# A fused attention and SoLU layer on one core: w_in's load moved ahead of chunk 1, late stores split over two queues, a new hand-off order

## Chip, core and metric

The kernel runs on one core of a Trainium2 chip. The metric is the time of one execution on the device in microseconds (us). Engines are named as in the profile: PE (TensorE, matmuls; PEld is its weight load), DVE (VectorE), ACT (ScalarE), POOL (GpSimd) and SP (SyncE, which here only issues DMAs). POOL and ACT issue DMAs as well.

## What is computed

```python
# q, k, v: (8, 8, 576, 64); w_in: (512, 1024); w_out: (1024, 512), all float32
kv = einsum('bhsd,bhse->bhde', k, v)
out = einsum('bhsd,bhde->bhse', q, kv)
x = out / sqrt(mean(out * out, -1) + 1e-6) * g_norm      # -> (4608, 512), heads side by side
h = x @ w_in
sm = softmax(h)                                          # with + 1e-9 in the denominator
solu = h * sm
ln = (solu - mean(solu)) / sqrt(var(solu) + 1e-6) * g_ln
y = ln @ w_out                                           # (4608, 512)
```

## The kernel before

The 4608 tokens are worked in nine chunks of 512. Chunks 0 to 7 take eight of every nine rows of one batch each (a partition holds nine rows in succession); chunk 8 (`LAST`) collects every ninth row of all batches, out of `q_last`. The kernel is a set of named steps, made by `add(name, engines, function, needs, uses)`. The string `ORDER` lists every step once, written out; `Plan.emit` walks it and issues each step on its engine, so every engine works through its own steps in exactly that order and never passes a step that waits. `word:act` in ORDER chooses ACT where a step may run on two engines. `HOME` gives each PSUM tile one of eight banks; two tiles of one bank follow each other, the second waits for the last reader of the first. `kept` gives the number of SBUF buffers by kind, and a load into a buffer waits for its last reader.

The steps of a chunk c, with the line of the profile that carries them:

- Loads `q.c`, `k.c`, `v.c` by POOL's DMA queue, which casts float32 to bf16 (L318). Chunks 0 and 1 come in halves of four heads (`HALVES`: `k.0.1` is the second half of chunk 0's k). The first halves of chunk 0 are loaded as float32 by SP (`ld.v`, `ld.k`, `ld.q`, L328) and cast by an engine (`v.0.0` and so on, L232). `w_in.0`, `w_in.1` are the halves of w_in (rows 0 to 255 and 256 to 511, L342), `w_out.0`, `w_out.1` those of w_out (L347). `gs` and `g_all` are small loads of the gains.
- `kv_mm` (L378) forms k-transposed times v; the `kv` steps copy it to bf16 (L232). `qT_mm` and `qT` transpose q by PE and copy it out (L416, L232); for chunks 5 to 8 (`XBAR`) one DMA transpose does it (`qT.5`, L425). `o_mm` (L444) multiplies the two.
- `sq` squares o (ACT, L236), `s_mm` (L508) takes the mean over each head, `ex` is the reciprocal root (ACT; chunk 0 in one step, L522, the others as Ln and Exp, `ln` L512 and `ex` L516), `x` multiplies it in (DVE, L528). For chunks 6 to 8 (`TOKA`) the same is done token by token: `o_mm` L458, `sq`, `ssum` (POOL), `sred` (DVE), `rh` (ACT), `rg` (POOL), `xt` (DVE), and a DMA transpose `x.c` (L500).
- `h.c.f` is x times w_in. In chunks 0 to 2 (`SPLIT`) `h.c.f.0` uses the first two of four blocks of the contraction (x's first half of heads, w_in.0) and `h.c.f.1` the last two (L583). `exp` (ACT, L590), `u` = h times exp (DVE, L594), `usq` (POOL or ACT) and `es` (POOL, L607) follow, then `sums` (PE, L694), `turn` and `stats` (DVE) and `rstd` (ACT). Chunks 4 to 8 (`TOKS`) keep tokens on the partitions: `h.c.m.g` (L612), `expt` (ACT, L620), `ut` (DVE, L626), `bn` (DVE, L632), `stats`, `rstd`, and a DMA transpose `turnu.c.half` (SP, L648) that gives the stationary operand of the last product.
- `w_mean` (PE, L741) and `w_center` (DVE, L746) fold g_ln and the mean into w_out, once.
- `out.c.m.part` is the product with w_out (L760), `ob` scales it by rstd (DVE L244 or ACT L242), `store` writes it out (L785, L788 and L783), all of them on SP but some of chunk 8. In chunks 6 and 7 one `store` issues two DMAs of 64 rows.

`warm.n` are filler matmuls on zeros (L824); `FILL` gives for each the bank that it writes, how many matmuls, and their columns.

## Time and profile before

| what | before |
|---|---|
| median of 3 runs | 183.58 us (183.0 to 183.73) |
| the profiled execution: its time | 184.51 us |
| its span, from the first to the last instruction | 182.4 us |
| busy: PE, DVE, ACT, POOL | 171.9, 133.5, 135.6, 98.0 us |
| first matmul of chunk 0's h | 20.80 us |
| end of the last matmul | 177.40 us |
| matmuls of `warm`: number, busy | 49, 14.80 us |
| HBM read, written | 32.54 MB, 9.44 MB |

Times inside the trace count from the first instruction of the span. The DMA share of a stretch can pass 1, since it sums the packets' own times. A row of the timeline gives the start, the duration, the engine and line, the operation with out<-in and shapes, how many are merged, and in brackets the idle time of that engine before it with what ended it.

### The profile page before, as it was taken

The page shows a single profiled execution, that of the slowest core. Times are in us where ns is not written, and L with a number is a line of the kernel's source. Part 1 is how long each engine was busy: PE and PEld are TensorE (multiplying, and loading weights), DVE is VectorE, ACT ScalarE, POOL GpSimd, SP SyncE. Part 2 cuts the span into 40 slices and gives each one's busy share as a digit, 9 for nine tenths or more (in the row PEclk, how much of TensorE's full clock was granted, in tenths as well). Part 3 has the DMA queues.
Part 4 walks back from the last instruction along what each step waited for, and adds up shares of the span by engine and source line. Part 5 has one row for each costly group of instructions (what it writes and reads, how often), then busy time and mean ns, then how long its engine had stood idle before and what let it go on. Part 6 is the DMA issues. An engine that isn't in the chain of part 4 may idle for free.

```text
span 182.4 us, 5075 instructions
## 1 busy us (share of the span) xinstructions
PE 171.9 (94%) x2057; PEld 83.7 (46%) x2074; DVE 133.5 (73%) x277; ACT 135.6 (74%) x279; POOL 98.0 (54%) x112
## 2 busy tenths in 40 slices
...
GB/s 188 291 213 211 207 313 324 205 210 207 209 207 269 244 207 209 207 193 149 254 131 91 167 127 156 114 205 202 218 167 163 252 262 185 208 140 216 207 239 170
DMA packets 56139, 37.10 MB, mean 203 GB/s; under 512 B 37548, under 2 KB 49332, under 8 KB 56116
## 3 DMA queue, kind: packets, MB, share of 16 engines
...
HBM read 32.54 MB, written 9.44 MB: 230 GB/s over the span
## 4 chain that ended last, share of the span: by engine, by line
PE 56%; DVE 12%; DMA 3%; ACT 1%; issue 1%
PE out_ps L760 22%; PE h_ps L612 17%; PE h_ps L583 8%; DVE bn_sb L632 4%; DVE u_sb L626 4%; DMA w_sb<-u_sb 3%; PE misc_ps L378 2%; PE misc_ps L694 2%; PE s_ps L508 2%; PE o_ps L444 1%; PE misc_ps L416 1%; DVE x_sb L528 1%; PE o_ps L458 1%; DVE w_out_sb L746 1%; DVE usq_sb L496 1%
## 5 line engine op out<-in xcount | busy, mean ns | idle before, releaser
L612 PE MATMUL h_ps<-w_in_sb,x_sb 128*128 128x512 bf16 x153 | 37.0, 379 | 0.8 <-DVE usq_sb L496 0.4
L760 PE MATMUL out_ps<-w_out_sb,w_sb 128*128 128x512 bf16 (+1 forms) x166 | 36.8, 369 | 0.6 <-DMA w_sb<-u_sb 0.3
L238 POOL TENSOR_TENSOR usq_sb<-u_sb 128x512 bf16<-128x512 bf16 x29 | 29.8, 1042 | 9.9 <-PE s_ps L508 6.4
L620 ACT ACTIVATE e_sb<-h_ps,zero_t 128x512 f32<-128x512 f32 x40 | 27.2, 687 | 8.5 <-PE h_ps L612 7.7
L583 PE MATMUL h_ps<-x_sb,w_in_sb 128*128 128x512 bf16 x128 | 30.4, 379 | 1.4 <-DVE x_sb L528 1.4
L760 PE MATMUL out_ps<-w_out_sb,u_sb 128*128 128x512 bf16 x120 | 30.4, 379 | 0.5
L594 DVE TENSOR_TENSOR u_sb<-h_ps,e_sb 128x512 bf16<-128x512 f32 x32 | 20.9, 685 | 8.8 <-ACT e_sb L590 8.7
L626 DVE TENSOR_TENSOR u_sb<-h_ps,e_sb 128x512 bf16<-128x512 f32 x40 | 26.0, 680 | 1.6 <-ACT e_sb L620 1.5
L632 DVE BATCH_NORM_STATS2 bn_sb<-u_sb 128x6 f32<-128x512 bf16 x40 | 25.8, 681 | 0.2
L760 PEld LDWEIGHTS <-w_sb 128*128 128x128 bf16 x168 | 16.3, 98 | 18.7 <-DMA w_sb<-u_sb 0.8
L612 PEld LDWEIGHTS <-x_sb 128*128 128x128 bf16 x160 | 15.4, 98 | 19.0 <-issue 1.2
L528 DVE SCALAR_TENSOR_TENSOR x_sb<-o_ps,g_cols,rst_sb 128x512 bf16<-128x512 f32 x24 | 18.8, 794 | 7.0 <-ACT rst_sb L516 3.8
L590 ACT ACTIVATE e_sb<-h_ps,zero_t 128x512 f32<-128x512 f32 x32 | 20.6, 691 | 4.2 <-PE h_ps L583 4.0
L607 POOL TENSOR_TENSOR es_sb<-e_sb 128x512 bf16<-128x512 f32 x16 | 20.2, 1274 | 2.2 <-ACT e_sb L590 2.2
L583 PEld LDWEIGHTS <-w_in_sb 128*128 128x128 bf16 x128 | 11.9, 98 | 15.8 <-issue 3.2
L760 PEld LDWEIGHTS <-u_sb 128*128 128x128 bf16 x128 | 11.9, 98 | 14.0 <-issue 0.8
L236 ACT ACTIVATE osq_sb<-o_ps,zero_t 128x512 bf16<-128x512 f32 x24 | 15.5, 682 | 3.4 <-PE o_ps L444 3.4
L489 POOL TENSOR_TENSOR lss_sb<-rh_sb,g_all 128x512 f32<-128x512 f32 x12 | 12.3, 1043 | 7.9 <-ACT rh_sb L485 7.9
L473 POOL TENSOR_TENSOR es_sb<-rst_sb 128x512 f32<-128x512 bf16 x6 | 6.9, 1157 | 15.3 <-ACT rst_sb L236 8.9
L512 ACT ACTIVATE lss_sb<-s_ps,eps_t 128x512 f32<-128x512 f32 x20 | 13.6, 685 | 1.7 <-PE s_ps L508 1.6
L516 ACT ACTIVATE rst_sb<-lss_sb,zero_t 128x512 f32<-128x512 f32 x20 | 14.5, 723 | 0.4
L232 DVE CAST kvd<-misc_ps 64x128 bf16<-64x128 f32 (+1 forms) x23 | 6.4, 288 | 9.1 <-PE misc_ps L378 7.7
...
## 6 DMA issues: line engine op xcount, KB each, us to landing
q_sb<-in_q_dram POOLq DMA_DIRECT2D x6, 576.0 KB, 18.1
k_sb<-in_k_dram POOLq DMA_DIRECT2D x6, 576.0 KB, 18.1
...
```

Of the source, the lines that this page charges most:

```text
L236: nc.scalar.activation(out=dst, in_=src, func=AF.Square, bias=zero_t[:, :])
L238: on[engine].tensor_tensor(out=dst, in0=src, in1=src, op=MUL)
L528: nc.vector.scalar_tensor_tensor(out=t[:, z, 2 * hf:2 * hf + 2].rearrange("p a (vt w) -> p w (a vt)", w=2), in0=T["o", c, hf, z].rearrange ...
L583: nc.tensor.matmul(bank(("h", c, f), [128, 512])[:, :], w_in_sb[:, dt, f * 128:(f + 1) * 128], T["x", c][:, :, dt, :], start=(dt == 0), st ...
L590: nc.scalar.activation(out=t[:, f % 2, :], in_=T["h", c, f][:, :], func=AF.Exp, bias=zero_t[:, :])
L594: nc.vector.tensor_tensor(out=t[:, f, :], in0=T["h", c, f][:, :], in1=T["e", c, f // 2][:, f % 2, :], op=MUL)
L607: on[engine].tensor_tensor(out=t[:, n, :], in0=e[:, 0, :], in1=e[:, 1, :], op=ADD)
L612: nc.tensor.matmul(bank(("h", c, m, g), [128, 512])[:, :], x[:, NP * (m ^ 2 * odd(c, dt)) + dt, :] if c in TOKA else x[:, m // 2 ^ odd(c, ...
L620: nc.scalar.activation(out=t[:, g, :], in_=T["h", c, m, g][:, :], func=AF.Exp, bias=zero_t[:, :], accum_out=se[:, m, g:g + 1])
L626: nc.vector.tensor_tensor(out=t[:, m, g * 512:(g + 1) * 512], in0=T["h", c, m, g][:, :], in1=T["e", c, m][:, g, :], op=MUL)
L632: nc.vector.bn_stats(out=t[:, m, g, :], in_=T["u", c][:, m, g * 512:(g + 1) * 512])
L760: nc.tensor.matmul(bank(key, [128, d_model])[:, cols], T["w", c][:, m, f, :] if c in TOKS else T["u", c][:, f, m * 128:(m + 1) * 128], w_o ...
```

## The change

In ORDER, SP loads `ld.v`, `ld.q`, `ld.k` one behind the other and then the small gains; POOL makes `ident` first, then loads `k.0.1`, `v.0.1`, `q.0.1`, then both halves of w_in, and only then chunk 1 and w_out; chunk 3's q comes ahead of chunk 2's. Chunk 0's first half of heads is worked first, then its second half. ACT casts v and q of that half, DVE casts k. The stores of chunks 6 and 7 become two steps each, `store.c.m.0` (64 rows) on SP and `store.c.m.1` on ACT (`store_part`), and stores of chunks 4 and 5 may go by ACT as well: ACT issues 17 stores instead of 3. The order of all other steps, the PSUM banks (`HOME`, all lines replaced) and the fillers (`FILL`, 44 matmuls instead of 49, 19 instead of 27 ahead of the first transposes) are new. The suffix "!" that FILL's words may have is not used in this FILL.

```diff
@@ -18,101 +18,102 @@
 ORDER = """
-warm.6 warm.3 ld.v q.0.1 ld.k k.0.1 v.0.1 ident warm.2 v.1.0 warm.0 q.1.0 qT_mm.0.1 v.0.0 k.0.0:act kv_mm.0.0 kv.0.0.0
-kv.0.0.1:act warm.1 k.1.0 qT.0.1:act gs w_in.0 w_in.1 k.1.1 ld.q q.0.0 qT_mm.0.0 warm.4 q.1.1 qT.0.0 kv_mm.0.1 turn_g
-o_mm.0.0 q_last.0:act sq.0.0.1 kv.0.1.1 kv.0.1.0 warm.7 s_mm.0.0.1 sq.0.0.0 ex.0.0.1 o_mm.0.1 sq.0.1.1 sq.0.1.0 g_ln
-s_mm.0.0.0 x.0.0.1 v.1.1 ex.0.0.0 warm.8 s_mm.0.1.1 ex.0.1.1 x.0.0.0 x.0.1.1 w_out.0 warm.12 s_mm.0.1.0 qT_mm.1.0
-qT.1.0 w_out.1 q.2.0 k.2.0 ex.0.1.0 x.0.1.0 v.2.0 kv_mm.1.0 kv.1.0.1:act kv.1.0.0:act warm.9 h.0.7.0 table h.0.1.0
-warm.5 h.0.4.0 o_mm.1.0 sq.1.0.0 sq.1.0.1 k.3.0 h.0.5.0 g_mean h.0.6.0 h.0.4.1 exp.0.4 u.0.4 usq.0.4 h.0.1.1 exp.0.1
-h.0.6.1 u.0.1 usq.0.1 h.0.5.1 exp.0.5 es.0.2 u.0.5 usq.0.5 exp.0.6 u.0.6 h.0.0.0 h.0.0.1 exp.0.0 u.0.0 q.3.0 usq.0.0
-s_mm.1.0.1 ln.1.0.1 ex.1.0.1 qT_mm.1.1 qT.1.1 usq.0.6 x.1.0.1 h.0.2.0 h.0.2.1 exp.0.2 u.0.2 s_mm.1.0.0 ln.1.0.0
...
-bn.8.2.0 turnu.8.0 out.7.0.0 out.7.0.1 ob.6.1:act out.7.2.0 store.6.1 bn.8.1.1 out.7.2.1 stats.7 rstd.7 out.7.3.0
-out.7.3.1 bn.8.0.1 ob.7.1 bn.8.1.0 ob.7.2:act store.7.2 out.8.2.0 out.8.2.1 out.8.1.0 out.8.1.1 out.8.0.0 out.8.0.1
-out.8.3.0 bn.8.0.0 bn.8.2.1 ob.7.3:act store.7.1 ob.7.0:act stats.8 rstd.8 ob.8.2:act ob.8.1:act store.7.3
-store.8.1:act ob.8.0:act store.8.0:act store.7.0 store.8.2 ob.8.3.0:act store.8.3.0 out.8.3.1 ob.8.3.1:act
-store.8.3.1:act
+ld.v ld.q ident k.0.1 ld.k k.0.0 v.0.1 gs v.0.0:act warm.0 q.0.0:act q.0.1 qT_mm.0.0 kv_mm.0.0 kv.0.0.1:act
+kv.0.0.0:act qT.0.0 warm.1 warm.2 o_mm.0.0 g_all w_in.0 w_in.1 v.1.0 sq.0.0.0 q.1.0 k.1.0 v.1.1 q.1.1 k.1.1 turn_g
+g_ln g_mean sq.0.0.1 kv_mm.0.1 s_mm.0.0.0 warm.3 s_mm.0.0.1 w_out.0 ex.0.0.1 kv.0.1.0 kv.0.1.1:act ex.0.0.0 qT_mm.0.1
+qT.0.1 warm.4 warm.5 o_mm.0.1 sq.0.1.0 warm.6 warm.7 s_mm.0.1.0 w_out.1 x.0.0.1 sq.0.1.1 x.0.0.0 h.0.7.0 h.0.3.0
+h.0.4.0 q.3.0 q.2.0 q_last.0:act ex.0.1.0 x.0.1.0 s_mm.0.1.1 ex.0.1.1 x.0.1.1 table h.0.6.0 h.0.1.0 h.0.0.0 h.0.2.0
+h.0.2.1 exp.0.2 h.0.3.1 exp.0.3 es.0.1 u.0.3 usq.0.3 h.0.4.1 exp.0.4 u.0.4 k.2.0 u.0.2 h.0.7.1 exp.0.7 u.0.7 v.2.0
+h.0.6.1 exp.0.6 u.0.6 usq.0.6 es.0.3 usq.0.4 h.0.1.1 exp.0.1 u.0.1 q_last.1 usq.0.1 qT_mm.1.0 qT.1.0:act usq.0.7
+h.0.5.0 h.0.5.1 exp.0.5 es.0.2 h.0.0.1 v.3.0 kv_mm.1.0 kv.1.0.1:act exp.0.0 es.0.0 kv.1.0.0 warm.8 warm.9 o_mm.1.0
+sq.1.0.1 warm.10 warm.11 s_mm.1.0.1 u.0.0 usq.0.0 u.0.5 usq.0.5 qT_mm.1.1 qT.1.1 sq.1.0.0 s_mm.1.0.0 ln.1.0.0
+kv_mm.1.1 kv.1.1.0 kv.1.1.1 warm.12 warm.13 o_mm.1.1 ln.1.0.1 ex.1.0.1 x.1.0.1 ex.1.0.0 x.1.0.0 k.3.0 k.5.0 v.5.0
+w_mean.0 sq.1.1.1 warm.14 s_mm.1.1.1 h.1.0.0 sq.1.1.0 ln.1.1.1 s_mm.1.1.0 ln.1.1.0 h.1.5.0 h.1.3.0 ex.1.1.0 x.1.1.0
+h.1.2.0 ex.1.1.1 x.1.1.1 w_mean.1 w_center.0 w_center.1 w_center.2 w_center.3 usq.0.2:act h.1.6.0 w_center.5 h.1.4.0
+h.1.4.1 h.1.6.1 exp.1.6 u.1.6 h.1.3.1 exp.1.3 exp.1.4 u.1.3 h.1.2.1 exp.1.2 u.1.4 h.1.0.1 exp.1.0 u.1.0 q.4.0 h.1.5.1
+usq.1.3 exp.1.5 u.1.5 u.1.2 usq.1.6 usq.1.2 sums.0 turn.0 w_center.4 qT_mm.3.0 qT.3.0:act usq.1.4:act es.1.2 out.0.0.0
+out.0.0.1 usq.1.5:act h.1.7.0 h.1.7.1 exp.1.7 es.1.3 u.1.7 stats.0 h.1.1.0 h.1.1.1 exp.1.1 u.1.1 es.1.0 out.0.3.0
+out.0.3.1 usq.1.1 es.1.1 qT_mm.2.0 qT.2.0:act k.4.0 qT_mm.3.1 usq.1.0 qT.3.1 out.0.3.2 kv_mm.2.0 kv.2.1.1:act
+kv.2.1.0:act kv.2.0.2 kv.2.0.1:act kv.2.0.0:act kv.2.1.2 rstd.0 qT_mm.2.1 qT.2.1 w_center.6 out.0.1.0 v.4.0 out.0.1.1
+out.0.0.2 w_center.7 o_mm.2.0 sq.2.0.1 o_mm.2.1 out.0.1.2 out.0.1.3 ob.0.1 out.0.3.3 ob.0.3 sq.2.0.0 usq.1.7
+s_mm.2.0.0 k.7.0 sq.2.1.0 ln.2.0.0 ex.2.0.0 out.0.0.3 ob.0.0 sq.2.1.1 s_mm.2.0.1 ln.2.0.1 ex.2.0.1 warm.15 kv_mm.3.0
+kv.3.1.2 kv.3.1.1 kv.3.1.0 kv.3.0.1:act out.0.2.0 v.7.0 out.0.2.1 out.0.2.2 x.2.0.0 v.6.0 kv.3.0.0 s_mm.2.1.0 ln.2.1.0
...
+ut.7.3.0 out.6.1.0 expt.7.0.0 ob.5.3:act out.6.1.1 bn.6.2.0 stats.6 ut.7.1.1 ut.7.0.0 x.8 h.8.2.1 bn.7.3.0 out.5.2.1
+turnu.7.0 bn.7.1.0 rstd.6 ob.6.2:act ob.6.1:act bn.7.2.1 expt.8.2.1 h.8.2.0 store.6.1.1 ut.8.2.1 out.6.0.0 out.6.0.1
+ut.7.2.0 h.8.3.1 h.8.1.0 expt.8.2.0 ut.8.2.0 expt.8.3.1 h.8.1.1 store.6.1.0 h.8.3.0 store.5.3:act bn.7.2.0 expt.8.1.1
+bn.8.2.0 bn.7.1.1 store.6.2.1 expt.8.3.0 store.2.3 h.8.0.1 expt.8.0.1 bn.7.3.1 store.6.2.0 ut.8.3.1 ut.8.3.0
+ob.5.2:act turnu.7.1 store.5.2 h.8.0.0 bn.8.3.1 ob.6.0:act ut.8.0.1 expt.8.0.0 bn.7.0.0 stats.7 out.6.3.0 ut.8.0.0
+out.6.3.1 ob.6.3:act turnu.8.1 expt.8.1.0 bn.8.2.1 ut.8.1.0 store.2.0 out.7.0.0 rstd.7 ut.8.1.1 bn.8.0.1 store.6.0.0
+turnu.8.0 out.7.1.0 out.7.1.1 bn.8.0.0 out.7.0.1 ob.7.0:act store.7.0.1 out.7.2.0 out.7.2.1 store.6.3.1 out.7.3.0
+out.7.3.1 ob.7.1 bn.8.1.0 store.7.1.1 store.6.0.1 store.7.0.0 store.7.1.0 out.8.2.0 out.8.2.1 ob.7.2 store.7.2.1
+out.8.1.0 out.8.1.1 ob.7.3:act store.7.3.0 out.8.0.0 bn.8.1.1 store.7.3.1 store.6.3.0 out.8.0.1 bn.8.3.0 stats.8
+rstd.8 ob.8.1 out.8.3.0 ob.8.2:act store.8.2:act store.8.1:act ob.8.0:act store.8.0:act store.7.2.0 out.8.3.1
+ob.8.3.1:act ob.8.3.0 store.8.3.1:act store.8.3.0
 """
...
 HOME = """
...
 """
...
-FILL = {0: ("s.warm", 19, 512), 1: ("misc.qT.0.0", 5, 512), 2: ("o.0.0.1", 5, 512), 3: ("o.0.1.1", 2, 512), 4: ("s.0.1.1", 1, 512), 5: ("h.0.4", 1, 512), 6: ("h.0.6", 1, 512), 7: ("s.0.0.1", 4, 512), 8: ("s.0.1.1", 2, 512), 9: ("h.0.7", 4, 512), 10: ("s.1.1.1", 1, 512), 11: ("h.1.1", 3, 512), 12: ("s.0.1.0", 1, 512)}
+FILL = {0: ("s.warm", 19, 512), 1: ("o.0.0.0", 2, 512), 2: ("o.0.0.1", 1, 512), 3: ("s.0.0.1", 1, 512), 4: ("o.0.1.0", 3, 512), 5: ("o.0.1.1", 1, 512), 6: ("s.0.1.0", 3, 512), 7: ("h.0.7", 1, 512), 8: ("o.1.0.0", 2, 512), 9: ("o.1.0.1", 1, 512), 10: ("s.1.0.1", 3, 512), 11: ("misc.qT.1.1", 1, 512), 12: ("o.1.1.0", 3, 512), 13: ("o.1.1.1", 1, 512), 14: ("s.1.1.1", 1, 512), 15: ("misc.kv.3.0.0", 1, 512)}
@@ -771,6 +772,10 @@
         t = kept_tile(ob_key(c, m), [128, d_model], FP32)
         times(engine, t[:, cols], T[key][:, cols], T["rstd", c][:, m:m + 1])
 
+    def store_part(engine, c, m, x):
+        rows = out[c * S:c * S + S, :].rearrange("(p j) d -> p j d", j=9)
+        on[engine].dma_start(rows[:, 4 * (m % 2) + m // 2 + 2 * x, :], T[ob_key(c, m)][64 * x:64 * x + 64, :])
+
     def store(engine, c, m, cols):
         t = T[ob_key(c, m)]
         first = 4 * (m % 2) + m // 2
@@ -781,11 +786,8 @@
                 on[engine].dma_start(last, t[:, cols])
             else:
                 on[engine].dma_start(out.rearrange("(r j) d -> j r d", j=9)[8, 128 * m:128 * m + 128, cols], t[:, cols])
-        elif c not in TOKA:
+        else:
             on[engine].dma_start(rows[:, first:first + 3:2, :], t[:, :])
-        else:
-            for x in range(2):
-                on[engine].dma_start(rows[:, first + 2 * x, :], t[64 * x:64 * x + 64, :])
 
     all_cols = slice(0, d_model)
     for c in range(NC):
@@ -808,7 +810,11 @@
                     [("w_center", f) for f in fs] + ([("turnu", c, m // 2)] if c in TOKS else [("u", c, f) for f in fs])
                     + ([("out", c, m, part - 1)] if part else []), [("w" if c in TOKS else "u", c), key])
             add(("ob", c, m), "dve|act", lambda e, key=key: scale(e, key, all_cols), [("out", c, m, n_parts - 1), ("rstd", c)], [key, ob_key(c, m), ("rstd", c)])
-            add(("store", c, m), "sp|act" if c == LAST else "sp", lambda e, c=c, m=m: store(e, c, m, all_cols), [("ob", c, m)], [ob_key(c, m)])
+            if c in TOKA and c < B:
+                for x in range(2):
+                    add(("store", c, m, x), ("sp", "act")[x], lambda _, a=(c, m, x): store_part(("sp", "act")[a[2]], *a), [("ob", c, m)], [ob_key(c, m)])
+                continue
+            add(("store", c, m), "sp|act" if c >= 4 else "sp", lambda e, c=c, m=m: store(e, c, m, all_cols), [("ob", c, m)], [ob_key(c, m)])
 
     def warm(key, n, cols):
         kind = key[1] if key[0] == "misc" else key[0]
@@ -827,10 +833,11 @@
 
     by_word = {plan.word(key): key for key in plan.users}
     for n, (word, count, cols) in FILL.items():
-        key = by_word.get(word, ("s", "warm"))
-        if key in plan.users:
-            plan.pieces[plan.users[key][0]][2].append(("warm", n))
-        add(("warm", n), "pe", lambda _, a=(key, count, cols): warm(*a), [], [key])
+        key, over = by_word.get(word.rstrip("!"), ("s", "warm")), word.endswith("!")
+        users = list(plan.users.get(key, []))
+        if users and not over:
+            plan.pieces[users[0]][2].append(("warm", n))
+        add(("warm", n), "pe", lambda _, a=(key, count, cols): warm(*a), users if over else [], [key])
 
     plan.settle(HOME)
     plan.emit(ORDER)
```

## The prediction

> **What bounds the kernel now.** I read first the head of the page and the busy time by stretches of the span (columns: length, then busy time of PE, its weight loads, DVE, ACT and POOL, granted clock, DMA share, GB/s), then the same view for the filler matmuls of L824 alone, then the timeline of the first 30 us.

> ```profile
> span 182.4 us, 5075 instructions
> 9.69:22.75 13.06, 12.06 (x293) 6.42 (x294) 6.51 (x12) 8.03 (x14) 4.66 (x7) 1.00 1.18 209
> 22.75:60.00 37.25, 35.51 (x487) 18.31 (x487) 27.35 (x50) 31.92 (x56) 35.40 (x38) 1.00 1.22 244
> 60.00:120.00 60.00, 59.47 (x935) 29.70 (x941) 48.65 (x95) 55.03 (x114) 38.67 (x40) 1.00 0.94 173
> 120.00:170.00 50.00, 49.25 (x283) 22.40 (x288) 48.33 (x102) 33.38 (x86) 11.76 (x12) 1.00 0.96 201
> 177.40:182.40 5.00, 0.00 (x0) 0.00 (x0) 0.00 (x0) 0.47 (x1) 0.00 (x0) 0.79 0.52 177
> 9.69:22.75 13.06, 5.05 (x18) 1.51 (x18) 1.00 1.18 209
> 20.80 1.02 PE L583 MATMUL h_ps<-x_sb,w_in_sb 128*128 128x512 bf16 x4 [0.46 <-DVE x_sb L528]
> 22.75 3.63 PE L583 MATMUL h_ps<-x_sb,w_in_sb 128*128 128x512 bf16 x16
> ```

> From 22.75 us on PE is busy for 35.51 of 37.25, 59.47 of 60 and 49.25 of 50 us: it is the bound, and no order of the same matmuls can take much out of that part. DVE (48.33 of 50 from 120 to 170 us) stands right beside it. What is left is the lead-in and the tail. Between 9.69 us and 22.75 us PE looks full with 12.06 us, but the second row of that stretch, which is L824's own, says that 5.05 us of it are fillers; before 9.69 us there are fillers alone. The first projection matmul of chunk 0 starts at 20.80 us, and the dense run, which needs both halves of w_in, at 22.75. After the last matmul come 5.00 us of stores.

> So the time is: the moment at which PE gets dense work, plus about 155 us of that work, plus 5 us. A change of the loads' order can move only the first term, and whatever starves PE later gives it back. What sets the first term is the POOL queue:

> ```profile
> 1.25 0.89 POOL L318 DMA_DIRECT2D q_sb<-in_q_dram  x1 [0.80 <-POOLq L851]
> 8.44 0.72 POOL L318 DMA_DIRECT2D k_sb<-in_k_dram  x1 [0.46 <-DMA q_sb<-in_q_dram]
> 12.33 0.72 POOL L318 DMA_DIRECT2D v_sb<-in_v_dram  x1 [0.67 <-DMA v_sb<-in_v_dram]
> 19.75 0.74 POOL L318 DMA_DIRECT2D k_sb<-in_k_dram  x1 [1.53 <-DMA w_in_sb<-in_moe_w_in_dram]
> 22.50 0.74 POOL L318 DMA_DIRECT2D v_sb<-in_v_dram  x1 [2.01 <-DMA w_in_sb<-in_moe_w_in_dram]
> 23.85 0.74 POOL L318 DMA_DIRECT2D k_sb<-in_k_dram  x1 [0.61 <-DMA k_sb<-in_k_dram]
> ```

> Each POOL load waits for the landing of the one eight places ahead of it, so these waits date the landings: the three second halves of chunk 0 between 8.44 and 12.33 us, w_in's halves at 19.75 and 22.50, k.1.1 at 23.85. Between 12.33 and 19.75 us the queue moves three loads of chunk 1 that nobody needs yet.

> **The loads at the start.** The change takes ld.q ahead of the small loads on SP, puts `ident` ahead of POOL's first load, and w_in behind the three second halves of chunk 0.

> ```profile
> 2.00:5.00 3.00, 3.00 (x9) 1.06 (x7) 0.27 (x1) 0.03 (x1) 2.85 (x8) 1.00 0.94 340
> q0 software_dynamic: 110, 0.13, 76.2%
> q1 hardware_dynamic: 83, 0.19, 55.0%
> q0 software_dynamic: 193, 0.20, 120.5%
> 3.56 0.22 POOL masks.py:197 MEMSET ident<- 128x128 bf16 x1
> 4.27 0.19 POOL masks.py:199 TENSOR_SCALAR_AFFINE_SELECT eye<-eye 9x9 f32<-9x9 f32 x1
> 4.73 0.96 DVE L232 CAST v_sb<-w_sb 128x1152 bf16<-128x1152 f32 x1 [3.03 <-DMA w_sb<-in_v_dram]
> ```

> The second to fourth rows are DMA queue totals (packets, MB, share) of the single microseconds 5 to 6, 8 to 9 and 11 to 12: POOL's queue q0 has no packet before 5.0 us, 3.75 us after its first issue; a microsecond shared leaves SP's q1 0.19 MB; q0 alone moves 0.20 MB per us as it lands in bf16. The four operations of `ident` span 3.56 to 4.46 us, 0.9 us, so POOL's packets now start at 5.9 us. SP alone moves 340 GB/s from 2 to 5 us, 1.02 MB, and some 0.36 MB more by 5.9; of its three loads of 0.59 MB, 0.39 MB are left, at 0.19 MB per us: ld.k lands at about 7.9 us, and the DVE cast of 0.96 us ends at 8.9.

> On q0 three loads instead of six stand ahead of w_in. The second halves still land by about 12.3 us (POOL starts later, but the engines carry SP's bytes meanwhile). Three halves of 0.295 MB at 0.20 are 4.4 us: w_in lands at 15.3 and 18.1 us. The end of chunk 1 does not move: the same bytes stand ahead of it in both orders, k.1.1 at 23.85 plus two more halves (2.9 us), about 26.7.

> **Chunk 0, in the new order.** The chain from 8.9 us, by these rows:

> ```profile
> 43.30 0.78 PE L378 MATMUL misc_ps<-v_sb,k_sb 64*64 64x64 bf16 x72
> 14.39 1.27 ACT L236 ACTIVATE osq_sb<-o_ps,zero_t 128x512 bf16<-128x512 f32 x2 [1.74 <-PE o_ps L444]
> 24.26 3.14 ACT L590 ACTIVATE e_sb<-h_ps,zero_t 128x512 f32<-128x512 f32 x5
> L512 ACT ACTIVATE lss_sb<-s_ps,eps_t 128x512 f32<-128x512 f32 x20 | 13.6, 685 | 1.7 <-PE s_ps L508 1.6
> L516 ACT ACTIVATE rst_sb<-lss_sb,zero_t 128x512 f32<-128x512 f32 x20 | 14.5, 723 | 0.4
> L528 DVE SCALAR_TENSOR_TENSOR x_sb<-o_ps,g_cols,rst_sb 128x512 bf16<-128x512 f32 x24 | 18.8, 794 | 7.0 <-ACT rst_sb L516 3.8
> 19.93 1.28 ACT L534 ACT_TABLE_LOAD   x1
> 57.25 3.45 PE h_ps L583 x16
> 35.87 0.79 DVE L528 SCALAR_TENSOR_TENSOR x_sb<-o_ps,g_cols,rst_sb 128x512 bf16<-128x512 f32 x1
> ```

> kv_mm.0.0 0.78, two small ACT casts 0.6, o_mm.0.0 0.4, two squares 1.27, one s_mm 0.4, then ex.0.0.1, a cast and ex.0.0.0 1.7: 14.1 us (o_mm, s_mm and the small casts are shorter than the kv_mm row; 0.3 to 0.4 each is my estimate). Two x of 0.79, the first beside the last ex, end at 14.9; w_in.0 at 15.3 is later. So the first h starts at 15.3 us, where it was 20.8. Beside it ACT does two squares, a copy and two ex, 3.0 us from 14.1 to 17.1, x.0.1.1 ends near 18, w_in.1 lands at 18.1: second halves from 18.4 us, against 22.75. By then seven h have their first half, 14 matmuls, against 6 matmuls before; against that, chunk 1's first kv, transposes and o (about 1.6 us) are not done. At 0.216 us (3.45 for 16) the 8 matmuls are 1.7, so the states are equal: **a lead of 4.3 us**.

> **What is given back at chunk 1.** Its loads are no earlier, and ACT is the chain. Table load to about 18.5, first exp at 19.0, six exps at 0.63 (3.14 for five) to 22.8, the copy of qT.1.0 1.0, one exp, one cast: 24.7; o_mm.1.0 to 25.1; exp and two squares 1.9, s_mm: 27.0. Two Ln and two Exp (685 and 723 ns) 2.8: 29.8, two squares 31.1, again two Ln and two Exp 33.9, x.1.1.1 at 34.7. Loads hide under that (k.1.1 and its like 26.7, w_out.0 another 1.05 MB of bytes that take about 2.6 us: 29.3, just ahead of w_mean.0's place). Before, the last x of chunk 1 ended at 36.66 (35.87 plus 0.79), with five h of chunk 1 half done; now six, 0.43 more: the lead is 2.0 + 0.4 = 2.4. The new fillers there (12 between kv_mm.1.0 and s_mm.1.1.1) sit in waits of PE and cost nothing while ACT is late.

> ```profile
> 39.59 2.06 DVE L746 SCALAR_TENSOR_TENSOR w_out_sb<-w_sb,g_cols,out_ps 128x512 bf16<-128x512 f32 x3
> 26.88 1.28 DVE L594 TENSOR_TENSOR u_sb<-h_ps,e_sb 128x512 bf16<-128x512 f32 x2
> 66.50 1.23 PE misc_ps L694 x80
> 48.32 1.24 PE out_ps L760 x5
> ```

> Next DVE is late: five w_center (0.69 each) go ahead of u.1.6, then six u (0.64 each) to 42.0, turn and w_center.4 to 43.1. PE reuses the banks of h.1 for qT_mm.3.0, out.0.0, out.0.3 and h.1.1, so it follows DVE; out.0.3 takes h.1.2's bank at 42.1, and kv_mm.2.0 ends at 45.0. Before, it ended at 44.08 (43.30 + 0.78). But by its place PE now has sums.0 (1.23) and five out pieces (10 matmuls, 2.2) behind it, 3.4 more: a lead of 2.5. The two places agree; I take **2.6 us** as what stays, between 0 (all given back, below) and 4.3 (none).

> **The rest of the order.** From here both kernels have the same PE work ahead, about 129 us of it (177.4 less 48.3). v.2.0 comes one full load later than before (q.3.0 is ahead of it): 26.7, w_out 5.2, four loads of 0.59 MB at 0.20, 11.6: 43.5 us, needed at 44.3. That holds with 0.8 us in hand. es.0.1 stands on POOL behind the issue of q.2.0, which waits for q.1.0 (about 20 us); its exps come no earlier. g_all's 32 KB go out early on SP and meet only SP's own idle time. DVE has three more ob, but in the stretch that DVE fills (120 to 170 us) three as before. Cost taken: nothing, with 1 us on either side, about what PE leaves idle from 60 to 170 us.

> **Stores and tail.**

> ```profile
> 172.00:176.00 4.00, 3.98 (x21) 2.06 (x22) 0.00 (x0) 1.56 (x3) 0.00 (x0) 1.00 0.90 199
> 176.00:180.00 4.00, 1.39 (x13) 1.00 (x11) 0.00 (x0) 1.32 (x3) 0.00 (x0) 1.00 0.93 316
> 166.79 2.76 SPq L648 DMA_TRANSPOSE w_sb<-u_sb  x1
> 172.02 5.37 PE L760 MATMUL out_ps<-w_out_sb,w_sb 128*128 128x512 bf16 x32 [0.34 <-DMA w_sb<-u_sb]
> L783 ACTq DMA_DIRECT2D out_dram<-v_sb x2: 338/356/374, 174.7 to 177.9; - x2
> ```

> SP issued turnu.8.0 at 166.79 us behind four stores, and PE waited 0.34 us for it at 172.02. Now some of those stores leave by ACT, but stats.7 and two bn stand ahead of ut.8.1.1 on DVE, about 1.5 us: no change. From 172 to 176 us stores go by SP's queue alone, 199 GB/s at a DMA share of 0.90; from 176 to 180 by SP's and ACT's, 316 GB/s at 0.93. Moving such halves on two queues from chunk 6 on could empty the tail sooner: at most 37% of 4 us, 1.5. Against it, store.2.3 and store.2.0 now come late, 0.5 MB. I take a gain of 0.2. [...]

> Added waits: 14 more stores are issued by ACT (17 against 3), at 0.36 us each, 5.0 us, and store.4.2, store.7.1.1 and store.7.2.1 wait there for DVE's ob with exps, rstd and ob behind them. ACT is busy for 33.38 of 50 us from 120 to 170: I hide them there.

> **Sum.** 182.4 - 2.6 - 0.2 = 179.6 us of span. The profiled execution took 184.51 us, 2.1 around its span and 0.93 above the median of 183.58; with both kept the forecast is **180.8 us**, 1.5% faster. Its own range is 179.0 to 182.5 (lead 4.3 or 1.1).

> **The rivals.** *Late loads of chunk 2.* If v.2.0 slips by more than 0.8 us, or k.3.0 behind it does, kv_mm.2.0 stands before out.0.1 and o_mm.2.0 on PE and everything waits. For it: the DMA share of 1.22 until 60 us, no reserve to catch up, and one load more ahead than before. Against it: the 0.8 us in hand, and POOL issues these loads well before they are due. It can take the whole lead: 183.4. The change's own claim can't fail much further, since fewer bytes stand ahead of w_in whatever the engines do.

> *ACT becomes the bound at the end.* The 14 issues fall between exps that DVE's ut waits for, and DVE has next to no idle time from 120 to 170 us; if none of the 5.0 us is hidden, 183.6 - 2.8 + 5.0 = 185.8. It decides from the point where more than 2.8 us of the 5.0 reach DVE. Against it: ACT's 17 us idle there. For it: ACT works in order, and each DVE-made ob that a store waits for stops the exps.

> *A cold PE.* Fillers ahead of the first transposes fall from 27 to 19. Eight at 0.216 less than the 9.69 us of before, PE is through with them by 8.0 and with the transposes by 8.6 at the latest, and then stands still until 8.9 us, longer if ld.k lands late. In the trace before the granted clock is 1.00 throughout and no such gap exists. If ld.k were 3 us late and the clock fell there, some 2 us of work until the fillers at 12 us would take twice as long: 182.6. [...]

> **How the numbers follow.** Forecast 0.57, late loads 0.17, ACT 0.21, cold PE 0.05. About 0.5% (0.9 us) is what a measurement of this kernel can tell from no change. Faster: 0.57 and 0.05, 0.62; same 0.17; slower 0.21. The range reaches down to 178.4 (lead 4.3 and a tail gain of 0.9) and up into the ACT case to 184.9, leaving out its upper end.

> **What would show it.** Right: the first h near 15.3 us and second halves from 18.4; the POOL waits dating w_in at 15 to 18 us; x.1.1.1 ending near 34.7; kv_mm.2.0 ending near 45; PE's last matmul near 174.8; a tail just under 5 us. Wrong: w_in landing at 15 us but PE idle or on fillers for over 5 us between 22 and 46 (the lead given back); DVE waiting for exps by more than 3 us after 120 us (ACT bound); PE idle before kv_mm.3.0; a granted clock under 1 in the first 20 us.

## The result and the profile after

| | before | after |
|---|---|---|
| median of 4 runs each on one chip, us | 183.29 (182.95 to 183.73) | 190.5 (188.51 to 192.22) |
| profiled execution, us (its span) | 184.51 (182.4) | 190.98 (189.2) |
| last matmul ends, us | 177.39 | 185.84 |
| from there to the end of the span, us | 5.0 | 3.35 |

After takes 1.0356 times as long, 95% interval 1.0265 to 1.0447 (this ratio leaves the run of 192.22 us out, the median does not): 7 us slower, where 2.8 us faster was forecast. The lines of after are 1 to 6 higher than those of before (h L584 and L613, out L761, x L529, fillers L830).

The start, in PE's timeline (columns: start, length, engine, line, operation, tiles, count, and in brackets the idle time ahead and what ended it):

```profile
10.70 0.78 PE L379 MATMUL misc_ps<-v_sb,k_sb 64*64 64x64 bf16 x72 [2.42 <-DVE k_sb L233]
19.40 4.48 PE L584 MATMUL h_ps<-x_sb,w_in_sb 128*128 128x512 bf16 x20 [0.74 <-DVE x_sb L529]
36.14 0.59 PE L584 MATMUL h_ps<-x_sb,w_in_sb 128*128 128x512 bf16 x2 [1.49 <-DVE x_sb L529]
47.62 0.78 PE L379 MATMUL misc_ps<-v_sb,k_sb 64*64 64x64 bf16 x72
```

and in those of ACT and DVE:

```profile
21.75 3.58 ACT L591 ACTIVATE e_sb<-h_ps,zero_t 128x512 f32<-128x512 f32 x6 [1.07 <-PE h_ps L584]
39.50 3.58 ACT L591 ACTIVATE e_sb<-h_ps,zero_t 128x512 f32<-128x512 f32 x6 [3.02 <-PE h_ps L584]
```

```profile
35.30 1.47 DVE L529 SCALAR_TENSOR_TENSOR x_sb<-o_ps,g_cols,rst_sb 128x512 bf16<-128x512 f32 x2 [2.38 <-ACT rst_sb L517]
37.70 3.38 DVE L747 SCALAR_TENSOR_TENSOR w_out_sb<-w_sb,g_cols,out_ps 128x512 bf16<-128x512 f32 x5 [0.94 <-PE out_ps L742]
41.00 3.67 DVE L595 TENSOR_TENSOR u_sb<-h_ps,e_sb 128x512 bf16<-128x512 f32 x6
```

The dense run of h does start 3.35 us sooner than before (19.40 against 22.75). It begins with the first halves of four h, as only three had theirs by then; the second halves follow at 21.12 (23.62 before). But the first exp comes at 21.75 (24.26 before), chunk 1's last x ends at 36.77 (36.66 before), and kv_mm.2.0 (the row at 47.62) ends at 48.4, where the kernel before has it at 44.08 with 3.4 us less work behind it.

The middle and the end, again PE's timeline; then a row of SP's issues, one of ACT's issues, and four microseconds of the busy time by stretches, with its columns as in the prediction (PE, PEld, DVE, ACT and POOL busy, then the granted clock, 1.00 for full speed, the DMA share and GB/s):

```profile
87.45 0.40 PE L695 MATMUL misc_ps<-es_sb,stat_sel 128*32 128x128 bf16 x13 [0.31 <-issue]
110.25 2.55 PE L761 MATMUL out_ps<-w_out_sb,u_sb 128*128 128x512 bf16 x11 [0.99 <-issue]
141.92 2.76 PE L613 MATMUL h_ps<-w_in_sb,x_sb 128*128 128x512 bf16 x12 [1.67 <-DMA x_sb<-usq_sb]
178.78 7.06 PE L761 MATMUL out_ps<-w_out_sb,w_sb 128*128 128x512 bf16 x32 [3.88 <-DMA w_sb<-u_sb]
```

```profile
171.25 4.19 SPq L649 DMA_TRANSPOSE w_sb<-u_sb  x1
```

```profile
172.49 3.64 ACTq L777 DMA_DIRECT2D out_dram<-k_sb  x2
```

```profile
180.00:184.00 4.00, 4.00 (x13) 1.54 (x12) 0.75 (x1) 0.67 (x1) 0.00 (x0) 0.62 0.61 216
```

turnu.8.0 is issued at 171.25 (before 166.79), SP takes 4.19 us to issue it (2.76), and it lands at 178.73 (171.97). PE stands still for 3.88 us, and then the granted clock is 0.62 from 180 to 184 us: the last 32 matmuls take 7.06 us (5.37 before). While SP issues the transpose, ACT takes 3.64 us to issue two stores.

To see where the time goes I gave each step of PE the time that its matmuls need back to back in the traces (0.216 us for 512 columns), left the fillers out, and asked at each moment when the kernel before had done the same sum. The table is worked out in this way from the matmul records, and is to be read to about half a microsecond; a plus is a lead over the profiled execution of before.

| at us | after | w_in_back | sp_and_turn | mended_both | no_fillers | tail_two_queues |
|---|---|---|---|---|---|---|
| 25 | +1.9 | -3.7 | +2.3 | +1.6 | +2.2 | +1.0 |
| 35 | -0.6 | -5.8 | -0.5 | -0.5 | -0.5 | +1.2 |
| 60 | -0.1 | -6.5 | +0.2 | +0.3 | +0.1 | +1.1 |
| 85 | +0.1 | -6.0 | +0.4 | +0.4 | +0.3 | +1.1 |
| 95 | -1.3 | -7.2 | -0.6 | -1.6 | -1.8 | +1.1 |
| 120 | -2.2 | -8.4 | -1.9 | -1.8 | -1.9 | +1.1 |
| 145 | -3.2 | -8.1 | -1.6 | -1.4 | -2.2 | +1.1 |
| 175 | -3.4 | -8.7 | -1.0 | -0.9 | -3.1 | +0.9 |

That execution of before was 0.9 us above its median and lost this at the start (the last column, whose start is before's own, is 1.0 to 1.2 us ahead of it from 15 us on), so against a median run every lead is about 1 us smaller. After wins 1.9 us, has lost them at 35 us, stays level to 85 us, loses 1.4 to 95 us, 0.9 to 120 us, 1.0 to 145 us and 5 behind 175 us; the tail, from the last matmul to the end of the span, gives 1.65 back.

### The profile page after: what moved, and what is told of

The parts are those of the page before. It is cut to its first block, busy times and chain, and to the rows that moved or that the text cites. A ratio compares the mean times of both kernels' runs of the same rounds, so it can differ in the third digit from the quotient of the medians.

```text
span 189.2 us, 5079 instructions
## 1 busy us (share of the span) xinstructions
PE 172.0 (91%) x2069; PEld 83.5 (44%) x2069; DVE 135.0 (71%) x281; ACT 135.6 (72%) x276; POOL 96.2 (51%) x111
## 4 chain that ended last, share of the span: by engine, by line
PE 71%; DMA 16%; ACT 7%; DVE 3%; issue 1%; SPq 0%; DVEq 0%
PE out_ps L761 24%; PE h_ps L613 17%; PE h_ps L584 14%; DMA w_sb<-in_k_dram 4%; DMA x_sb<-usq_sb 4%; DMA w_sb<-u_sb 4%; DMA qT_sb<-q_sb 3%; PE misc_ps L379 3%; PE s_ps L509 2%; PE misc_ps L417 2%; ACT rst_sb L517 2%; PE o_ps L830 2%; PE o_ps L445 2%; ACT lss_sb L513 2%; ACT osq_sb L237 2%; PE misc_ps L695 1%
## 5 line engine op out<-in xcount | busy, mean ns | idle before, releaser
L761 PE MATMUL out_ps<-w_out_sb,w_sb 128*128 128x512 bf16 (+1 forms) x168 | 38.4, 381 | 3.9 <-DMA w_sb<-u_sb 3.9
L613 PE MATMUL h_ps<-w_in_sb,x_sb 128*128 128x512 bf16 x160 | 37.0, 379 | 1.7 <-DMA x_sb<-usq_sb 1.7
L239 POOL TENSOR_TENSOR usq_sb<-u_sb 128x512 bf16<-128x512 bf16 x27 | 27.8, 1039 | 18.4 <-DVE u_sb L595 18.3
L584 PE MATMUL h_ps<-x_sb,w_in_sb 128*128 128x512 bf16 x128 | 30.3, 379 | 2.4 <-DVE x_sb L529 2.4
L761 PE MATMUL out_ps<-w_out_sb,u_sb 128*128 128x512 bf16 x128 | 31.2, 379 | 1.0 <-issue 1.0
L761 PEld LDWEIGHTS <-w_sb 128*128 128x128 bf16 x168 | 16.7, 100 | 23.6 <-DMA w_sb<-u_sb 4.4
L529 DVE SCALAR_TENSOR_TENSOR x_sb<-o_ps,g_cols,rst_sb 128x512 bf16<-128x512 f32 x24 | 18.6, 792 | 9.2 <-ACT rst_sb L517 7.3
L613 PEld LDWEIGHTS <-x_sb 128*128 128x128 bf16 x160 | 15.5, 98 | 20.6 <-DMA x_sb<-usq_sb 2.2
L584 PEld LDWEIGHTS <-w_in_sb 128*128 128x128 bf16 x128 | 11.9, 98 | 17.5 <-issue 3.7
L761 PEld LDWEIGHTS <-u_sb 128*128 128x128 bf16 x128 | 11.8, 98 | 15.2 <-issue 2.2
L490 POOL TENSOR_TENSOR lss_sb<-rh_sb,g_all 128x512 f32<-128x512 f32 x12 | 12.3, 1042 | 5.4 <-ACT rh_sb L486 5.3
L517 ACT ACTIVATE rst_sb<-lss_sb,zero_t 128x512 f32<-128x512 f32 x20 | 14.1, 721 | 0.5
L243 ACT ACTIVATE k_sb<-out_ps,rstd_sb 128x512 f32<-128x512 f32 x10 | 6.7, 685 | 6.4 <-PE out_ps L761 6.2
```

The lines of the kernel that those rows point to most:

```text
L239: on[engine].tensor_tensor(out=dst, in0=src, in1=src, op=MUL)
L529: nc.vector.scalar_tensor_tensor(out=t[:, z, 2 * hf:2 * hf + 2].rearrange("p a (vt w) -> p w (a vt)", w=2), in0=T["o", c, hf, z].rearrange ...
L584: nc.tensor.matmul(bank(("h", c, f), [128, 512])[:, :], w_in_sb[:, dt, f * 128:(f + 1) * 128], T["x", c][:, :, dt, :], start=(dt == 0), st ...
L613: nc.tensor.matmul(bank(("h", c, m, g), [128, 512])[:, :], x[:, NP * (m ^ 2 * odd(c, dt)) + dt, :] if c in TOKA else x[:, m // 2 ^ odd(c, ...
L761: nc.tensor.matmul(bank(key, [128, d_model])[:, cols], T["w", c][:, m, f, :] if c in TOKS else T["u", c][:, f, m * 128:(m + 1) * 128], w_o ...
```

## The experiments

The theory: the start's lead is real but spent in chunk 1, and the loss comes from the end, where DMA transposes are issued late (order) and are slow beside stores on ACT's queue. The rivals: the order alone, the queue alone, the start alone, ACT as the bound.

**The end: sp_stores.** All 13 stores of chunks 4 to 7 that ACT issues go to SP.

```diff
-store.4.2:act store.4.1:act store.4.0:act store.5.0:act store.5.3:act
+store.4.2 store.4.1 store.4.0 store.5.0 store.5.3
-    add(("store", c, m, x), ("sp", "act")[x], ...
+    add(("store", c, m, x), "sp", ...
```

> The changed kernel with one thing undone: the 13 stores of chunks 4 to 7 that ACT issues go back to SP, at the same places of the order, halves still apart. Queue theory (stores on ACT's queue make SP's transposes slower to issue and to land): turnu.8.0's issue falls from 4.19 us to about 2.8, its landing from 7.48 to 5.2, x.7's landing from 8.03 to about 6; PE's waits of 3.88 and 1.67 us shrink by 2 to 3 us together, the wait at the end is too short for the clock to fall, and the time comes near 186. Order theory (the transposes are late because of where the new order puts DVE's and SP's steps): landings as before or later, because SP now has more to issue ahead of them; 190 to 193. My rival of the prediction (ACT is the bound): ACT gets rid of 5 us of issues and the time falls by 2 us or more although the transposes land no sooner.

188.85 us, ratio to before 1.027 (1.0222 to 1.0319). SP's and PE's timelines and the chain of waits:

```profile
170.55 2.83 SPq L647 DMA_TRANSPOSE w_sb<-u_sb  x1
```

```profile
140.50 2.76 PE L611 MATMUL h_ps<-w_in_sb,x_sb 128*128 128x512 bf16 x12 [0.33 <-DMA x_sb<-usq_sb]
175.06 5.37 PE L759 MATMUL out_ps<-w_out_sb,w_sb 128*128 128x512 bf16 x32 [1.58 <-DMA w_sb<-u_sb]
```

```profile
170.55 4.46 DMA w_sb<-u_sb
```

The queue theory's numbers came: issue 2.83, landing 4.46 us, both waits of PE shrink by 3.6 us together and the granted clock stays at 1.00 up to the last matmul. The gain in time is smaller, since the stores now end the kernel: 5.5 us from the last matmul to the end of the span of 185.9. ACT as an engine was not the bound: freed of its issues it gained nothing that PE waited for.

**keep_clock.** 16 fillers ahead of out.8.1.

```diff
+16: ("out.8.1", 16, 512)    # in FILL
-out.8.1.0
+warm.16 out.8.1.0
```

> The changed kernel with 16 filler matmuls (3.5 us) ahead of out.8.1, in the bank that out.8.1 is about to take: they fill most of PE's last wait of 3.88 us and do no useful work. If the halved pace of the matmuls behind that wait (0.427 us each from 178.8 to 183.1 us) is the clock falling for want of work, the granted clock stays at 1.00, the last 32 matmuls take 5.4 us where they took 7.06, and the time falls by 1.5 to 2 us, to about 188.7. If the pace came from the weights' landing or from DMA traffic, nothing changes: 190 to 191.

189.25 us, ratio 1.028 (1.0229 to 1.0331).

```profile
179.80 5.37 PE L759 MATMUL out_ps<-w_out_sb,w_sb 128*128 128x512 bf16 x31 [0.90 <-DMA w_sb<-u_sb]
```

5.37 us again, with a granted clock of 1.00 from 180 to 184 us: the slow pace is the clock, it follows the standstill, and it costs 1.7 us on these matmuls. The time fell by 1.25 us, less than the 1.5 to 2 expected: out.8.1 starts 1.0 us later in this execution than in after's. Of after's own four runs the one whose mean clock was 1.000 took 188.51 us.

By the trace of after alone the length of the stop could decide: 3.88 us did it, 2.42 us at the start did not. Others here do not fit that. The first two rows, of start_of_after and start_mended (below), follow stops of 2.50 and 2.08 us and show a lowered clock; the third, of start_mended2, follows one of 3.07 us and does not:

```profile
61.00:65.00 4.00, 3.96 (x12) 1.54 (x13) 0.35 (x1) 1.58 (x3) 0.85 (x2) 0.62 1.15 276
11.00:15.00 4.00, 3.95 (x94) 2.28 (x93) 1.16 (x3) 1.60 (x4) 2.12 (x3) 0.57 1.19 214
180.00:184.00 4.00, 3.39 (x16) 1.58 (x17) 0.75 (x1) 1.28 (x3) 0.00 (x0) 1.00 0.86 273
```

**turn_first and sp_and_turn.** Three stores go from ahead of the last transposes to behind them; the second run adds sp_stores.

```diff
-store.5.2 ... turnu.8.1 ... store.2.0 ... store.6.0.0 turnu.8.0
+turnu.8.1 ... turnu.8.0 store.5.2 store.2.0 store.6.0.0
```

> The changed kernel with three stores on SP's queue (store.5.2, store.2.0, store.6.0.0) moved from ahead of turnu.8.1 and turnu.8.0 to right behind turnu.8.0; engines and queues of all stores as in the change. Order theory: turnu.8.0 is issued when ut.8.1.1 is done (169.4 us) and not at 171.25, so out.8.1 starts 1.8 us sooner, PE's wait falls to about 2 us, the clock does not fall, and the time drops by 3 to 4 us, to about 187. Queue theory: the transpose is issued sooner but then has the same ACT stores beside it, takes 7 us or longer to land, and no more than 1 to 2 us is won: 189.

> Both cures of the end together: the 13 stores of chunks 4 to 7 on SP (alone 188.85) and the three stores behind turnu.8.0 (alone 187.92). If slow landing (queue) and late issue (order) are two causes, x.7 comes 1.2 us and turnu.8.0 3 to 4 us sooner, PE has no wait at the end, and the time is 186 to 186.8. If they are one and the same 3.9 us of wait, whichever cure takes it, the time stays near 188 and the tail behind the last matmul grows instead, to over 5.5 us, as the stores that were moved back then end the kernel.

turn_first 187.92 us, ratio 1.0212 (1.0181 to 1.0243); together 186.94, ratio 1.0195 (1.0119 to 1.0271). SP's timeline of the first, PE's and the chain of the second:

```profile
160.92 10.08 SPq L647 DMA_TRANSPOSE w_sb<-u_sb  x3
```

```profile
162.70 15.72 PE L759 MATMUL out_ps<-w_out_sb,w_sb 128*128 128x512 bf16 x79
```

```profile
175.27 3.62 DMA out_dram<-v_sb
```

With the three transposes back to back PE waits for none of them at the end, with or without the ACT queue. So late issue and slow landing are two causes of one wait, and either cure takes most of it. In turn_first turnu.8.0 has two ACT stores beside it all the same, and is issued in 1.98 us (ut.8.1.1, which it needs, ends at 168.65, the row above at 171.00) and lands in 4.9: ACT's stores do not slow every transpose. In sp_and_turn the last matmul ends at 178.4, 7.4 us before after's, but 6.4 us then pass to the end of the span: the stores moved back end the kernel, as the second case of its expectation had it, and the sum is 3.6 us better than after, not 7.

**w_in_back.** w_in's loads go back behind chunk 1's first halves, nothing else.

```diff
-w_in.0 w_in.1 v.1.0 sq.0.0.0 q.1.0 k.1.0
+v.1.0 sq.0.0.0 q.1.0 k.1.0 w_in.0 w_in.1
```

> The changed kernel with its first part undone and nothing else: w_in's two loads go back behind the first halves of chunk 1's v, q and k, as in the kernel before. If w_in's early load is worth what I forecast (4.3 us at h, 2.6 kept), h starts some 3 to 4 us later and the whole kernel is 2.5 us or more slower: 193. If it is worth nothing, because chunk 1's attention then sets the pace (its k and v come 3 us sooner here): h starts later, x.1.1.1 and kv_mm.2.0 come within 0.5 us of where they were, and the time stays at 190 to 191.

197.5 us, ratio 1.0741 (1.0659 to 1.0822).

```profile
21.13 2.74 PE L582 MATMUL h_ps<-x_sb,w_in_sb 128*128 128x512 bf16 x6 [4.34 <-DMA w_in_sb<-in_moe_w_in_dram]
```

By the table the early w_in is worth 5.6 us at 25 us and 6.1 at 85 us, more than I forecast, but only in this order, which does nothing else on PE until h can start. Part of this is the clock: h starts 4.15 us later (16.98 in after), and behind the stop of 4.34 us the granted clock is 0.50 from 21 to 25 us, so that six matmuls take 2.74 us (1.46 in after). The kernel before had chunk 1's first attention steps there, and stands level without an early w_in.

**The lead: h1_first, start_mended, start_mended2, mended_both.** The stretch from 33 to 45 us in three other orders; the last adds the cures of the end. The core of the second mend:

```diff
-x.1.1.0 h.1.2.0 ex.1.1.1 x.1.1.1 w_mean.1 w_center.0 ... w_center.3 h.1.6.0 w_center.5 h.1.4.0 h.1.4.1 h.1.6.1 exp.1.6
+h.1.2.0 w_mean.1 ex.1.1.0 x.1.1.0 ex.1.1.1 x.1.1.1 w_center.0 h.1.3.1 exp.1.3 h.1.2.1 exp.1.2 w_center.1 u.1.3
```

> The changed kernel with one stretch of its order mended, from 34 to 47 us: w_mean.1 goes ahead of the last Exp of chunk 1, and after x.1.1.1 the second halves come first whose first halves are done (h.1.3, 1.2, 1.0, 1.5), where the change starts h.1.6 and h.1.4 from the beginning; w_center is spread among the u. If the lead was lost to this order, the first exp of chunk 1 comes at about 37 us where it came at 39.5, sums.0 and kv_mm.2.0 come 1.5 to 2.5 us sooner, and the time falls by as much, to about 188.5. If DVE (w_center and u) or the landing of chunk 2's k and v sets the pace there, kv_mm.2.0 stays near 47.6 us and the time at 190 to 191.

> The changed kernel with the stretch from 33 to 45 us put in another order, and now nothing ahead of w_mean.1 that waits for x.1.1: h.1.2.0 and w_mean.1 go ahead of x.1.1.0, the four h of chunk 1 that have their first halves get their second halves first, four of the six w_center go behind the u, and four banks are given so that PE follows DVE's new order. If the lead is lost to the order of this stretch, PE's wait of 1.49 us at 36.1 goes, the first exp of chunk 1 comes near 37.3 (39.50 in the change), kv_mm.2.0 near 46.4 (47.7), and the time falls by about 1.2 us, to 189.3. If chunk 1 is held by ACT (without a gap from 21.75 to 36.5 us) and then by DVE whatever the order, kv_mm.2.0 stays and the time is 190 to 192.

> The changed kernel with the stretch from 33 to 45 us mended a second time, now with only the banks of h.1.3 and h.1.6 swapped (and out.0.3 taken ahead of out.0.0), so that nothing behind 50 us is touched. If the order of this stretch costs the lead: the first exp of chunk 1 near 37.3 us, useful work on PE 1.2 us further on from 40 us to 85 us than in the change, and the time near 189.3 against 190.5. If ACT and the loads hold it: no difference at 50 us and 190 to 191.5.

> The same mend together with both cures of the end (stores of chunks 4 to 7 on SP, three of them behind turnu.8.0; without the mend 186.94). If the losses add up as separate waits: 185.5 to 186. Then 2 us are left against the kernel before, from 87 to 120 us. If what the start gains is taken back later (PE arrives sooner at transposes that are no sooner there): 186.5 to 187.5.

h1_first 191.59 us (PE waits for u.1.6's bank, which my order gave it), start_mended 194.67 (189.88 to 196.5, too wide for a ratio; banks given elsewhere cost 2.5 us at 65 to 70), start_mended2 188.43, ratio 1.0265 (1.0229 to 1.03), mended_both 186.33, ratio 1.0151 (1.0116 to 1.0186). Why start_mended2 is 2 us below after stays open: its trace is of an execution of 191.1 us, and on top of the cures of the end the same mend changes the time by 0.6 us (186.33 against 186.94), within the intervals. From ACT's and PE's timelines of mended_both:

```profile
37.80 3.71 ACT L589 ACTIVATE e_sb<-h_ps,zero_t 128x512 f32<-128x512 f32 x6 [1.02 <-PE h_ps L582]
47.21 0.78 PE L377 MATMUL misc_ps<-v_sb,k_sb 64*64 64x64 bf16 x72
```

The exps come 1.7 us sooner than in after, kv_mm.2.0 by 0.4, no more. In the table mended_both and sp_and_turn are alike from 35 to 85 us. So my second theory, that the order of these steps spends the lead, falls. It could not have held: by the table the lead is gone at 35 us, where this stretch begins. What fills the time ahead of it is ACT, which runs from 21.75 to 36.5 us with no gap over 0.62 us. In its timeline of before, and then of after:

```profile
22.86 1.26 ACT L236 ACTIVATE osq_sb<-o_ps,zero_t 128x512 bf16<-128x512 f32 x2 [1.65 <-PE o_ps L444]
```

```profile
25.18 1.04 ACT L233 COPY qT_sb<-misc_ps 128x1024 bf16<-128x1024 bf16 x1
27.48 1.26 ACT L237 ACTIVATE osq_sb<-o_ps,zero_t 128x512 bf16<-128x512 f32 x2
```

Before, ACT had chunk 1's first two squares done ahead of its first exp, and DVE made the copy of qT.1.0. Now both, and a cast of kv.1 (0.32 us), stand behind the first exp on ACT: 2.6 us together, about the 2.5 us by which the first exp comes sooner (21.75 against 24.26). That this is where the lead went is argued: no run moves these steps back.

**no_fillers.** Without warm.8 to warm.14.

> The changed kernel without the seven groups of fillers from 25 to 33 us (14 matmuls, 3 us of PE time) that stand between chunk 1's attention steps. If they lie in waits that are there anyway, kv_mm.2.0 comes where it was and the time is 190 to 191; if the clock falls without them, the matmuls after 30 us take up to twice as long and it is 191.5 to 193; if they hold up useful work, 188.5 to 189.8.

188.6 us, ratio 1.0284 (1.0236 to 1.0332).

```profile
47.39 0.78 PE L376 MATMUL misc_ps<-v_sb,k_sb 64*64 64x64 bf16 x72
```

kv_mm.2.0 comes 0.23 us sooner, and so did the dense run (19.16): the fillers lie in waits and cost nothing there. The median is the one expected had they held up work, but not for that reason: the difference in the traces arises at 145 and 175 us, where the transposes land. Whether leaving the fillers out moved these landings, or executions differ there by themselves, stays open.

**Halves of the change: start_of_after, rest_of_after, start_fixed.** After's steps up to kv_mm.2.0 and then before's; the reverse; and the first with h1_first's mend and two queues.

> The change's start alone: its order, banks and fillers up to and with kv_mm.2.0 (about 48 us), and from there on the steps of the kernel before that are left, in the order, banks and with the stores of before (two banks of chunk 2 swapped so that the two halves fit). Theory of the lost lead: what h wins at 19.4 us is gone when chunk 1's attention is through, useful work on PE stands 1 us behind the kernel before from 35 us on, and the time is 183.5 to 185. My prediction's step (a lead of 2.6 us is kept): 180.5 to 181.5. Whatever this is above 183.6, the rest of the 6.9 us lies behind 48 us.

> The other half: order, banks and fillers of the kernel before up to and with kv_mm.2.0, then what is left in the change's order with its banks and its stores on two queues (two banks swapped so that the halves fit). Theory of the order behind (turnu.8.0 and x.7 late, PE idle at 140 and 175 us, then the clock): nearly all of the loss is here, 188 to 190. If the losses behind 48 us only pass on what the start loses, it comes to 183.5 to 185.

> Put together: the start of the change with the stretch mended as in the run just above, then the order of the kernel before, with the stores of chunks 6 and 7 by halves on two queues. If each part does what its theory says: 183.6, less 0.4 (stores), and 1.5 us on either side for the start with its mend: 181.5 to 183. If the start cannot keep a lead whatever its order is (loads of chunk 2, ACT from 21.75 to 36.5 us without a gap): 183.5 to 184.5.

192.73, 197.36 and 194.79 us: each worse than either kernel. PE's timeline of the first:

```profile
61.04 1.89 PE L758 MATMUL out_ps<-w_out_sb,u_sb 128*128 128x512 bf16 x4 [2.50 <-DVE x_sb L526]
```

In the first the loss is at the seam, 7.7 us between 47 and 65 us. Part of it is the clock (0.62 from 61 to 65 us, shown above); for the rest I argue that loads, w_center and banks of the one half do not meet what the other expects. In rest_of_after some 2 us are lost at the seam and more later, at stops of 2.78 and 4.62 us with a lowered clock behind each (0.50 from 114 to 116 us and from 186 to 188 us). This order could not be split in two here; these runs tell nothing of the parts.

**The stores alone: two_queues, turn_ahead, tail_two_queues.** The kernel before with the stores of chunks 6 and 7 by halves on SP and ACT; with turnu.8.0 ahead of store.6.3 and store.5.0; with the latter and two queues only for stores behind that transpose.

```diff
-... store.6.3 ... store.5.0 bn.8.2.0 turnu.8.0
+... bn.8.2.0 turnu.8.0 store.6.3.0 store.6.3.1 store.5.0
-            add(("store", c, m), ...
+            if (c, m) in ((6, 1), (6, 3), (7, 0), (7, 1), (7, 2), (7, 3)):
+                for x in range(2):
+                    add(("store", c, m, x), ("sp", "act")[x], ...
```

> One part of the change alone: the kernel before, in its own order, with the stores of chunks 6 and 7 by halves, rows 0 to 63 of each tile by SP and rows 64 to 127 by ACT, in place of both by SP. Queue theory: transposes that have ACT stores beside them land later than the 5.18 us of turnu.8.0 before, and ACT loses 8 issues of 0.5 us or more among the exps; 1 to 3 us slower than before, 184.5 to 186.5, in spite of a shorter tail. Order theory: SP has 8 fewer issues ahead of its transposes and the last stores leave on two queues: same or up to 1 us faster, 182.3 to 183.3.

> The kernel before with one thing changed: turnu.8.0 goes ahead of store.6.3 and store.5.0 on SP's queue; all stores as before on SP. If the gain of 1.06 us with two queues as well came from the tail: PE's wait of 0.34 us goes, the tail stays 5 us, 183.1 to 183.4. If it came from turnu.8.0's place: 182.3 to 182.7.

> The kernel before with only the stores behind its last transpose on two queues: turnu.8.0 goes ahead of store.6.3 and store.5.0, and the stores of 6.1, 6.3 and chunk 7 leave by halves, SP and ACT. No such store can meet a transpose. If two queues empty the tail sooner (5.0 us behind the last matmul before, 3.7 with all of chunks 6 and 7 on two queues), PE's wait of 0.34 us goes and the tail takes 3.7 us or less: 182.0 to 182.6, 0.6 to 0.9% faster. If the tail is held by the bytes that are left (DMA share 0.90 to 0.93), 183 to 183.6.

two_queues 183.22 us, ratio 0.9968 (0.9941 to 0.9995); turn_ahead 183.86, ratio 0.9997 (0.997 to 1.0023); tail_two_queues 182.37, ratio 0.9942 (0.9919 to 0.9965), faster than both kernels. SP's timeline and the chain of two_queues, then PE's of turn_ahead (span 180.9) and of tail_two_queues (span 180.1):

```profile
165.84 4.05 SPq L647 DMA_TRANSPOSE w_sb<-u_sb  x1
```

```profile
165.84 6.16 DMA w_sb<-u_sb
```

```profile
161.75 14.00 PE L758 MATMUL out_ps<-w_out_sb,w_sb 128*128 128x512 bf16 x72
```

```profile
171.08 5.37 PE L759 MATMUL out_ps<-w_out_sb,w_sb 128*128 128x512 bf16 x32 [0.49 <-DMA w_sb<-u_sb]
```

The same effect in the other kernel: beside ACT's stores the transpose takes 4.05 us to issue and 6.16 to land, where it took 2.76 and 5.18. It costs 0.3 us there, because PE had work. The tail falls from 5.1 us (180.9 less 175.75) to 3.65 (180.1 less 176.45). Taking PE's wait away alone gives nothing; the two queues behind the last transpose give the 1.06 us. In the tail of before SP issues one store of 128 KB every 0.62 us, about 210 GB/s:

```profile
172.20 2.47 SPq L788 DMA_DIRECT2D out_dram<-v_sb  x4
```

That this pace was the limit is argued. The runs show that the tail is about 1.5 us shorter with half of these stores on a second queue.

**stores_early and small_apart.** Chunk 2's four stores right behind their ob; and, on top of sp_and_turn, sums.2 and o_mm.6 moved apart from other small matmuls.

```diff
-sums.2 turn.2 out.2.1.0 ... out.2.1.1
+out.2.1.0 ... out.2.1.1 sums.2 turn.2
-sums.3 o_mm.6.0 ... o_mm.6.1 out.3.3.0 out.3.3.1
+sums.3 out.3.3.0 o_mm.6.0 ... out.3.3.1 o_mm.6.1
```

> The changed kernel with chunk 2's four stores right behind their ob (about 84 to 90 us), where it has them at 113, 132, 160 and 170 us, between the transposes of the end; nothing else moved. If the late stores hold up the transposes and the tail (1.0 MB out of the way, SP's queue 0.6 us shorter ahead of x.7, turnu.7.1 and turnu.8.0): x.7 lands about 1 us sooner, turnu.8.0 1 to 2 us sooner, PE's waits shrink by as much and the time falls to 187.5 to 189. If the transposes wait for DVE's and ACT's order or are slow by ACT's stores alone, 190 to 191.

> The changed kernel with both cures of the end (stores of chunks 4 to 7 on SP, three of them behind turnu.8.0; 186.94 without more) and two steps of PE moved: sums.2 (80 small matmuls) goes behind out.2.1, so that it no longer follows kv_mm.7.0 and kv_mm.6.0 (72 each) at once, and out.3.3's halves go between sums.3, o_mm.6.0 and o_mm.6.1 (80, 32 and 32). If PE stops there because its instructions are not fetched fast enough (a fetch of 16 KB by the DMA queue of instructions begins 2.2 us ahead of the end of each stop), both stops go and the time falls by 1 to 2 us, to 185 to 186. If the stops come from a wait that the records do not show, they stay or move with the steps: 186.5 to 187.5.

stores_early 190.81 us, ratio 1.0378 (1.0311 to 1.0446); small_apart 188.53, ratio 1.024 (1.0182 to 1.0298). PE's timeline of each:

```profile
110.88 1.07 PE L457 MATMUL o_ps<-kvd,qT_sb 64*64 64x64 bf16 x64 [3.52 <-DMA qT_sb<-q_sb]
180.78 5.37 PE L759 MATMUL out_ps<-w_out_sb,w_sb 128*128 128x512 bf16 x32 [1.68 <-DMA w_sb<-u_sb]
```

```profile
87.22 1.02 PE L759 MATMUL out_ps<-w_out_sb,u_sb 128*128 128x512 bf16 x4 [1.04 <-DVE u_sb L593]
```

The early stores take 2.2 us off the last wait and put 3.5 us on qT.6, with a granted clock of 0.50 from 110 to 114 us: qT.6's transpose stands on SP's queue behind these stores, and is issued at 105.44 where after has it at 100.68. In small_apart both stops without a releaser are gone, but PE now waits for DVE in their place, and its 188.53 us lie above both cases of its expectation and above the 186.94 of sp_and_turn: what stands behind these stops stays open.

## Why the prediction was wrong

Against the forecast span of 179.6 us the trace has 189.2, 9.6 us more: 2.5 from the lead that was not kept, 3.3 from 85 to 145 us, 5.2 from there to the last matmul, less 1.45 that the tail gained beyond the forecast.

- **First h and lead at h (4.3 us).** Right in kind, too large: h started at 16.98 (15.3), its second halves at 21.12 (18.4), against 23.62 before (I had misread 22.75, where a first half starts). The first term that was off is ld.k: it landed at 9.86 us, 8.1 after its issue, where I had 7.9 us on the clock from bytes and shares. The trace before had the nearer row: the third load of SP, q's, took 7.6 us. From 8 to 9 us SP's queue moved 0.05 MB, where I had 0.19 per us. K's cast ended 1.7 us late, and the chain of chunk 0 with it. The second is the count of first halves: three were done when the dense run began, not seven, and the other four (8 matmuls, 1.7 us) stood ahead of the first second half.
- **Lead kept (2.6 us).** This step failed. The chain from the first exp to chunk 1's last x took 15.0 us against my 15.7, but it began 2.75 us late (21.75, not 19.0): 1.7 from k's cast, 1.0 from the four first halves, for which ACT waits 1.07 us in the row at 21.75. The lead at that point was to be 2.4 and was nothing (36.77 against 36.66 before). What DVE does next was costed rightly in length and not in start. The prediction was right that chunk 1 gives lead back and that ACT sets its pace, and wrong on how much. No order that I tried kept more than half a microsecond of it.
- **The rest of the order (0, within 1).** It cost 3.3 us from 85 to 145 us: two stops of PE in dense runs of small matmuls (0.31 and 0.99 us), a wait of 0.65 us at 92.49 for qT.6's transpose, and the 1.67 us for x.7. My 1 us was what PE left idle before, which says nothing of a new order.
- **turnu.8.0 "no change".** The largest error, 5 us, and this step failed too. I counted stats.7 and two bn ahead of ut.8.1.1 against fewer stores ahead of the transpose, and neither the two transposes near each other on SP nor that the last is slower beside ACT's stores. It was issued 4.5 us later and took 7.48 us to land, not 5.18. In the profiled execution of before PE already waited 0.34 us for it, so there was no slack: any delay went straight to PE, and the stop of 3.88 us then to the clock, 1.7 us more.
- **Tail (gain 0.2).** The 0.2 was a choice that no run shows. The tail gained 1.65, near the upper bound of 1.5 that I had worked out and set aside. Part of this may be luck: stores could drain while PE stood still for 3.88 us, and in turn_first, with two queues and no such stop, but with stores moved back, the tail takes 7.6 us. The time saved can be SP's issue time. The row of four stores in 2.47 us fits that; that it was all of the gain is not shown.
- **Rivals.** Late loads of chunk 2 did not happen: PE waits for none of them. ACT as the bound had the right sign and the wrong mechanism: ACT's stores go with a slower last transpose on SP (4.19 us to issue, 2.83 without them in sp_stores); ACT itself waited 5.67 us for a slot at 176 us. A cold PE at the start did not come in this execution, with a gap of 2.42 us, but by little: stores_early, start_mended, start_fixed and start_mended2 have the same first steps, and there stops of 1.98 to 2.77 us were followed by half the clock. So a gap like this one was enough in four runs, and my chance of 0.05 for this rival was an estimate that no run bears out. In after it came at the end, where I had not looked.

Not settled: the two stops of PE recorded as issue, and whether ACT's steps ahead of 36 us are what holds chunk 1.
